# Four modulation rows: summed on the tensor engine in 32-column tiles and spread by DMA, and one operand difference moved from VectorE to GpSimd

## The chip, the core and the metric

The kernel runs on one core of a Trainium2 chip. The metric is the device time of one execution in microseconds (us). The core has five engines that each run their own instruction stream in order and meet through semaphores: TensorE (PE in the profile, with its weight loads as PEld), VectorE (DVE), ScalarE (ACT), GpSimd (POOL) and SyncE (SP), which here only issues DMAs. All matrix products write to PSUM; VectorE and ScalarE read PSUM, GpSimd does not in this kernel.

## What is computed

One transformer block for 2048 tokens of width 576, conditioned on a vector `c`. Everything is float32.

```python
mod = (silu(c) @ w_mod).reshape(1, 6, 1, 576)
sa, ca, ga, sb, cb, gb = (mod[:, i] for i in range(6))
h = layernorm(x) * (1 + ca) + sa
x = x + ga * attention(h)          # 32 query heads of width 18, one shared key/value head, then @ wo
h = layernorm(x) * (1 + cb) + sb
y = layernorm(h)
x = x + gb * (gelu(y @ w1 + b1) @ w2 + b2)   # hidden width 4608
```

The six vectors `sa ... gb` are rows of 576 numbers: one product of `silu(c)` with a slice `w_mod[:, 576 j : 576 (j + 1)]` each. The change concerns four of them: `ga` (j = 2), `sb` (3), `cb` (4) and `gb` (5). The other two are made in the first 20 us in another way and are not touched.

## The kernel before

**Stages.** From 0 to about 125 us: layernorm, queries, keys, values and the first score maxima. From about 125 to 1390 us: attention in 32 "quads" of four heads times 512 tokens (8 quads for each block of 512 tokens, `NQT` = 32). From 1390 to 2241 us: the MLP in 36 steps `v` (18 groups of 256 hidden units, first for one pair of token blocks, `v` = 0 to 17, then for the other pair, `v` = 18 to 35). Each step makes the two products of a 2 x 2 block matrix scheme with seven block products (`A11 S2 S3 A12 S1 A22 S4`), and their operands are sums and differences of blocks of the normalized activations.

**The order in a quad** is written by hand: the strings `QUAD` and `QUADW` list S (score products, line 901, exponentials on ScalarE, line 903), M (score maxima for the next quad, line 319, reduced on VectorE, line 923), X and R (another piece of the maxima), V (the product of probabilities with the values, line 891: four matmuls with 32 output columns each, one for each head of the quad, which write four 32-partition strips of one PSUM bank). PSUM tiles rotate: four named `psB`, three `psM`, one `psC`. After every second key block (every second `kc`, eight times in a quad) `between` takes one step of a generator from the queue `fill`. The first generator in that queue is `late_weights` (from line 493).

**`late_weights`** makes the four rows. For each row, `wmod[j]` is loaded as five blocks of 128 x 576 (line 527 for j = 5, 2, 3; line 92, `load_mod`, for j = 4). GpSimd multiplies each by its column of `silu(c)` (`scaled`, line 498) and adds the five blocks up (`added`, line 501), so that one 128 x 576 tile remains whose sum over the 128 partitions is the row. `bcast` (line 516) makes that sum and copies it to all partitions at once: a matmul with a 128 x 128 matrix of ones (`unity`), in two halves of 288 columns (line 521), each into a `psB` tile of its own, and VectorE scales, adds a constant and writes the result (line 522), to `gab` (`ga`) or to a row of `BC` (0: `sb`, 1: `1 + cb`, 2: `gb / 2`). The loop from line 532 runs 12 steps of `late_weights`: two steps of the sums each, and from the seventh on, in each second one, one `bcast`. Then `wmod[4]` and `wo` are loaded, the sum and the `bcast` for j = 4 follow, and GpSimd multiplies `wo` by `gab` and splits it in two parts (lines 550 to 552), one of five blocks a step.

**Who uses the rows.** `gab`: line 550 at once. `BC[:, 2]`: the preparation of the MLP's weights (line 799), which starts in the fifth quad. `BC[:, :2]`: the second layernorm, from the second token block on.

**The change of pairs.** In the step `v` = 17 the operands of the other pair are formed by `form` (line 1010), a few at a time between the block products. `+X` copies an operand to its rounded form (ScalarE, line 1023), `-X` makes the rest that rounding left out (VectorE or GpSimd, line 1025), and `=X` makes an operand as a difference of two blocks of `yr` (line 1016): `=T3`, `=T4` and `=T1`. `=T4` overwrites the block that `-B21` reads, so it comes after it. Here `e2` is GpSimd; at the first pair (`v` = 0) `e2` is VectorE. While this goes on, TensorE finishes the output products of step 16 (`fc2`, line 1248), whose `psA` tiles (two in rotation) are added to the residual by VectorE at line 1285; the gelu of each block runs over lines 1120, 1121 (ScalarE), 1123 (VectorE), 1124 (ScalarE), 1126 (VectorE), 1129 (ScalarE) and 1132 (GpSimd); lines 1380, 1389 and 1402 add block products on VectorE.

Of the kernel before, what the change touches and what calls it, by code (L numbers as in the profile page):

```python
# [8 lines left out]
F32 = mybir.dt.float32  # L9
F32R = mybir.dt.float32r  # L10
AF = mybir.ActivationFunctionType
ALU = mybir.AluOpType
AX = mybir.AxisListType

S, D, H, DH, F = 2048, 576, 32, 18, 4608
# [17 lines left out]
def block_kernel(ctx: ExitStack, tc, x, wqkv, wo, w1, b1, w2, b2, c, wmod, ident_in, out):  # L33
    nc = tc.nc
    ve, ac, po, pe, sy = nc.vector, nc.scalar, nc.gpsimd, nc.tensor, nc.sync

    per = ctx.enter_context(tc.tile_pool(name="per", bufs=1))
    dr = ctx.enter_context(tc.tile_pool(name="dr", bufs=1, space=bass.MemoryType.DRAM))
# [14 lines left out]
    def psB(): return PS["t"].tile([128, 512], F32, name="psB", bufs=PS["b"])  # L53
# [3 lines left out]
    def big(): return per.tile([128, 10, 512], F32R, name="big", bufs=3)  # L57

    def bigw(n):
        return per.tile([128, KD, n], F32, name="bigw", tag="big", bufs=3, padded_shape=[128, KD, 1024])  # L60
# [14 lines left out]
    BC = per.tile([128, 3, D], F32, name="BC")  # L75
# [14 lines left out]
    def load_mod(j):  # L90
        t = bigw(D)
        sy.dma_start(t, wmod[j])
        return t
# [18 lines left out]
    unity = pa.tile([128, 128], F32, name="unity")  # L112
# [373 lines left out]
    px = pxp.__enter__()  # L486
# [3 lines left out]

    WO, YR, ATT, B2 = {}, {}, {}, {}

    def late_weights():

        gab = pb.tile([128, D], F32, name="gab", tag="r2", bufs=3)

        def scaled(w, k0, k1):
            po.tensor_tensor(w[:, k0:k1], w[:, k0:k1], st[:, k0:k1, None].to_broadcast([128, k1 - k0, D]), op=ALU.mult)

        def added(w, k0, k1, n=1):  # L500
            po.tensor_tensor(w[:, k0:k0 + n], w[:, k0:k0 + n], w[:, k1:k1 + n], op=ALU.add)

        def total(w):

            scaled(w, 0, 2)
            yield
            scaled(w, 2, 4)
            yield
            scaled(w, 4, 5)
            added(w, 0, 2, 2)  # L510
            yield
            added(w, 0, 1)
            added(w, 0, 4)
            yield

        def bcast(w, dst, add, scl):

            for h2 in range(2):
                cs = slice(288 * h2, 288 * (h2 + 1))
                p = psB()  # L520
                pe.matmul(p[:, :288], unity, w[:, 0, cs], start=True, stop=True)
                ve.tensor_scalar(dst[:, cs], p[:, :288], scl, add, op0=ALU.mult, op1=ALU.add)
            yield

        m3, m2, m5 = (bigw(D) for _ in range(3))
        for j, t in ((5, m5), (2, m2), (3, m3)):
            sy.dma_start(t, wmod[j])
        yield
        sums = (x for t in (m5, m2, m3) for x in total(t))
        rows = (x for a in ((m5, BC[:, 2, :], 0.0, 0.5), (m2, gab, 0.0, 1.0), (m3, BC[:, 0, :], 0.0, 1.0))  # L530
                for x in bcast(*a))
        for i in range(12):
            for _ in range(2):
                next(sums, None)
            if i > 5 and i % 2:
                next(rows)
            yield
        m4 = load_mod(4)
        wor = bigw(D)
        sy.dma_start(wor, wo)  # L540
        ATT[0] = big()
        yield
        yield from total(m4)
        yield
        yield
        yield from bcast(m4, BC[:, 1, :], 1.0, 1.0)
        wos = pw.tile([128, 2, KD, D], F32R, name="wos", tag="wA", padded_shape=[128, 2, KD, WQC])
        WOH, WOL = WO["h"], WO["l"] = wos[:, 0], wos[:, 1]
        for k in range(KD):
            po.tensor_mul(wor[:, k, :], wor[:, k, :], gab)  # L550
            po.tensor_copy(WOH[:, k, :], wor[:, k, :])
            po.tensor_tensor(WOL[:, k, :], wor[:, k, :], WOH[:, k, :].bitcast(F32), op=ALU.subtract)
            yield
# [312 lines left out]
    P, PVt = {}, {}  # L866
    posts = []
    fill = deque([late_weights()])

    def step(q):  # L870
# [79 lines left out]
    for n in range(NQT):  # L950
# [13 lines left out]
        for tok in order:  # L964
            if tok[0] == "V":
                g = int(tok[1])
                while g:
                    i = min(g, 4 - pq % 4)
# [36 lines left out]
    def op_pieces(R, e2):  # L1005


        at = {"B11": (0, 0, ve), "B21": (2, 2, e2), "B22": (4, 7, e2), "T2": (6, 5, ve), "T1": (8, 5, ve),
              "T3": (10, 0, ve), "T4": (12, 2, e2), "t0": (0, 4, ve), "t1": (1, 9, ve)}
        less = {"T3": (5, 0, 0), "T4": (2, 5, 2), "T1": (7, 5, 5)}  # L1010

        def form(what):
            for w in what.split():
                if w[0] == "=":
                    x, y, o = (R[:, i:i + 2] for i in less[w[1:]])
                    (e2 if w == "=T1" else ve).tensor_tensor(o, x, y, op=ALU.subtract)
                    continue
                a, r, e = at[w[1:]]
                n = 2 if w[1] in "BT" else 1
                o, lo = (OP, 14) if n == 2 else (TL[0], 2)  # L1020
                hi, src = o[:, a:a + n], R[:, r:r + n]
                if w[0] == "+":
                    ac.activation(hi, src, AF.Copy)
                else:
                    e.tensor_tensor(o[:, lo + a:lo + a + n], src, hi.bitcast(F32), op=ALU.subtract)
        return form
# [31 lines left out]
    px = ctx.enter_context(tc.tile_pool(name="mx", bufs=1, side="right", reuse_waits="tile"))  # L1058
# [256 lines left out]
    for v in range(NV):  # L1315
# [44 lines left out]
        bc = psB()  # L1360
# [111 lines left out]
```

## Time and profile before

| | us |
|---|---|
| median of 3 runs (2241.82 to 2245.19) | 2242.26 |
| the profiled execution's own time | 2243.08 |
| its span, which the profile divides up | 2241.3 |

The profile is of one execution; its times count from the start of the span, so the execution's own time is 1.8 us more than its span. The granted clock of TensorE was 0.998 over the span.

| engine | busy, us | share of the span |
|---|---|---|
| PE | 2212.7 | 99% |
| PEld | 1442.2 | 64% |
| DVE | 1940.8 | 87% |
| ACT | 1645.1 | 73% |
| POOL | 1524.7 | 68% |

Matmuls are pipelined and their ends are modelled, so that PE counts as busy nearly always; where it loses time is read from the starts of its rows. In a row of the timeline stand the start in us, the time from the first start to the last end in us, the engine, the line, the operation, the tile written and the tiles read, for matmuls the rows and columns of the weights, the shape and the count; in brackets the engine's idle time before the row and what ended it. In a row of the table of windows stand the window, its length, and for each engine the busy time and the number of instructions.

### The profile page before, as it was taken

The numbers are of one execution on the slowest core, as the hardware profiler recorded it, in microseconds if no ns is written. First come the engines' busy times: TensorE is split into PE (matmuls) and PEld (weight loads), VectorE is DVE, ScalarE is ACT, GpSimd is POOL, SyncE is SP. The second block draws the span as 40 slices with busy tenths as digits, with TensorE's granted clock in tenths as the row PEclk, the third lists the DMA queues.
The fourth block names the chain that finished last, engine by engine and source line by source line (L and its number), as shares of the span: only waits on it lengthen the run. The fifth ranks groups of instructions, "written<-read, shape, count | busy, mean of one in ns | idle before, by whom it ended". The sixth has DMA issues, their size and how long they took to land.

```text
span 2241.3 us, 45781 instructions
## 1 busy us (share of the span) xinstructions
PE 2212.7 (99%) x16458; PEld 1442.2 (64%) x16458; DVE 1940.8 (87%) x3420; ACT 1645.1 (73%) x3145; POOL 1524.7 (68%) x1760
## 2 busy tenths in 40 slices
PE   7999999999999999999999999999999999999999
PEld 5644544444444544444444445888888888989898
DVE  7589999999999999999999982887888878888787
ACT  5569999999999999999999997444545544344443
POOL 6654356776877787777776300888888857877776
PEclk9999999999999999999999999999999999999999
DMA  6232034443433333343333101666666646676664
GB/s 229 85 129 75 15 114 138 133 142 110 138 121 126 121 122 115 124 139 115 117 127 127 49 13 48 194 177 179 180 178 176 190 122 181 182 213 191 177 183 125
DMA packets 182404, 303.79 MB, mean 136 GB/s; under 512 B 19243, under 2 KB 74923, under 8 KB 182177
## 3 DMA queue, kind: packets, MB, share of 16 engines
q1 hardware_dynamic: 182033, 300.72, 42.9%
q8 instruction: 130, 2.13, 0.4%
q14 instruction: 97, 0.79, 0.1%
q10 hardware_dynamic: 144, 0.15, 0.0%
HBM read 198.71 MB, written 93.19 MB: 130 GB/s over the span
## 4 chain that ended last, share of the span: by engine, by line
PE 86%; DVE 3%; ACT 3%; POOL 2%; issue 1%; DMA 0%; SPq 0%; POOLq 0%; ACTq 0%
PE psC L891 21%; PE psB L1111 18%; PE psA L1214 16%; PE psB L901 13%; PE psM L319 10%; PE psB L700 2%; ACT P L903 2%; PE psB L911 2%; DVE mx L923 1%; PE psA L1248 1%; PE psA L700 1%; DVE xc L921 0%; PE psB L155 0%; PE psB L357 0%; PE psB L248 0%
## 5 line engine op out<-in xcount | busy, mean ns | idle before, releaser
L903 ACT ACTIVATE P<-psB 128x512 f32<-128x512 f32 x2008 | 1043.8, 619 | 35.0 <-PE psM L319 12.3
L923 DVE TENSOR_REDUCE mx<-psM 128x1 f32<-128x512 f32 x1476 | 938.1, 683 | 37.5 <-PE psM L319 14.9
L319 PE MATMUL psM<-KS,qst 64*128 64x512 f32 x1722 | 601.2, 442 | 0.4 <-DVE mx L923 0.4
L901 PE MATMUL psB<-qst,KS 64*128 64x512 f32 x2008 | 585.1, 429 | 1.7 <-DVE mx L337 1.5
L891 PE MATMUL psC<-P,V 128*32 128x256 f32 (+3 forms) x6424 | 576.3, 448 | 0.5 <-ACT O L715 0.5
L901 PEld LDWEIGHTS psB<-qst,KS 64*128 64x128 f32 x2008 | 303.4, 185 | 218.2 <-ACT P L903 141.3
L1111 PE MATMUL psB<-ops,w1a 128*128 128x512 f32 x1512 | 393.8, 396 | 0.2 <-DVE h L1126 0.2
L319 PEld LDWEIGHTS psM<-KS,qst 64*128 64x128 f32 x1722 | 275.6, 184 | 161.9 <-DVE mx L923 120.4
L1111 PEld LDWEIGHTS psB<-ops,w1a 128*128 128x128 f32 x1512 | 270.1, 188 | 46.6 <-DVE h L1126 0.6
L891 PEld LDWEIGHTS psC<-P,V 128*32 128x32 f32 x6424 | 140.0, 108 | 200.1 <-issue 173.4
L1220 DVE TENSOR_TENSOR XT<-psA,XT 128x576 f32<-128x576 f32 x330 | 241.7, 753 | 19.0 <-PE psA L1214 13.6
L1214 PEld LDWEIGHTS psA<-w2s,big 128*128 128x128 f32 x1584 | 223.0, 188 | 13.9 <-POOL big L1188 2.5
L1214 PE MATMUL psA<-w2s,big 128*128 128x288 f32 x1584 | 230.4, 294 | 0.0
L1124 ACT ACTIVATE psB<-gs 128x512 f32<-128x512 f32 x144 | 86.7, 602 | 130.0 <-DVE gs L1123 130.0
L1188 POOL TENSOR_TENSOR big<-s,big 128x512 fp32r<-128x512 f32 x132 | 170.9, 1295 | 10.6
L1120 ACT ACTIVATE h<-psB,b1t 128x512 f32<-128x512 f32 x144 | 97.9, 680 | 102.5 <-PE psB L1111 81.8
L921 DVE CUSTOM_DVE_ANT_0 xc<-psM,xc 128x512 f32<-128x512 f32 x246 | 165.8, 680 | 3.6 <-PE psB L901 1.5
L914 ACT ACTIVATE xc<-psB 128x512 f32<-128x512 f32 x246 | 152.8, 621 | 8.8 <-PE psM L319 7.4
L735 POOL TENSOR_TENSOR os<-O,os 128x512 fp32r<-128x512 f32 x28 | 36.1, 1289 | 164.8 <-ACT os L734 164.8
L1123 DVE SCALAR_TENSOR_TENSOR gs<-psB,h 128x512 f32<-128x512 f32 x144 | 98.5, 684 | 39.5 <-ACT psB L1121 39.4
L762 POOL TENSOR_TENSOR r<-r,r 128x256 fp32r<-128x256 f32 (+1 forms) x162 | 121.6, 751 | 13.0
L1129 ACT ACTIVATE big<-h 128x512 fp32r<-128x512 f32 x39 | 24.7, 633 | 133.7 <-DVE h L1126 133.7
(214 smaller groups left out, 3341.2 us busy)
## 6 DMA issues: line engine op xcount, KB each, us to landing
w1a<-w1scr SPq DMA_DIRECT2D x252, 256.0 KB
w2s<-w2sum SPq DMA_DIRECT2D x132, 288.0 KB
w1scr<-r SPq DMA_DIRECT2D x126, 256.0 KB
w2s<-w2scr SPq DMA_DIRECT2D x76, 288.0 KB
w2scr<-r SPq DMA_DIRECT2D x72, 288.0 KB
w2sum<-r SPq DMA_DIRECT2D x72, 288.0 KB
qst<-qscr SPq DMA_DIRECT2D x192, 72.0 KB
w1a<-w2scr SPq DMA_DIRECT2D x33, 288.0 KB
```

The lines of the kernel that those rows point to most:

```text
L319: pe.matmul(o, QST[n][64 * g:64 * g + 64, p, 128 * qt:128 * (qt + 1)], KS[64 * g:64 * g + 64, 512 * kb:512 * (kb + 1)], start=True, stop=True)
L762: po.tensor_tensor(o[:, n:2 * n], src, o[:, :n].bitcast(F32), op=ALU.subtract)
L891: pe.matmul(PVt[n][32 * j:32 * (j + 1), cs], V[:, kc, :], t[:, j, cs], start=(kc == 0 and h0 == 0), stop=(kc == 15), skip_group_check=True)
L901: pe.matmul(t, KS[64 * g:64 * g + 64, 128 * kc:128 * (kc + 1)], QST[n][64 * g:64 * g + 64, i, :], start=True, stop=True)
L903: ac.activation(P[n, kc][:, 2 * i + g, :], t, AF.Exp, scale=SCALE)
L914: ac.activation(XC[-1], t, AF.Relu)
L921: ve.tensor_tensor_reduce(c, t, c, 1.0, -3.0e38, ALU.add, ALU.max, o)
L923: ve.tensor_reduce(o, t, axis=AX.X, op=ALU.max)
L1111: pe.matmul(o, x, y, start=(first and i == 0), stop=(i == len(terms) - 1), skip_group_check=True)
L1188: po.tensor_tensor(unit(u, 1), x, unit(u, 0).bitcast(F32), op=ALU.subtract)
L1214: pe.matmul(p[:, i, :288], x[:, ts_], W2S[k][:, y], start=(bool(first) and q == 0), stop=(q == 2), skip_group_check=True)
L1220: ve.tensor_tensor(o, p[:, :, :288], o, op=ALU.add)
```

## The change

Four edits, in the code's order. A row of DRAM is set aside for each of the four vectors. `bcast` is rewritten: in place of two matmuls of 128 output columns by 288 it issues four of 32 output columns by 144, the j-th for the j-th quarter of the row, into the j-th 32-partition strip of one `psB` tile (the form that line 891 has); VectorE evacuates 128 x 144 into a small tile; one DMA writes one partition of each strip, 4 x 144 numbers, to the DRAM row; after a `yield`, another DMA reads that row into all 128 partitions of the target. Since `bcast` now yields twice, the loop steps it in each of its last six rounds instead of in each second one. And in `form`, `=T4` goes to `e2` as `=T1` does, so only `=T3` stays on VectorE.

```diff
+    rowscr = [dr.tile([1, D], F32, name="rowscr%d" % n) for n in range(4)]
...
-        def bcast(w, dst, add, scl):
-
-            for h2 in range(2):
-                cs = slice(288 * h2, 288 * (h2 + 1))
-                p = psB()
-                pe.matmul(p[:, :288], unity, w[:, 0, cs], start=True, stop=True)
-                ve.tensor_scalar(dst[:, cs], p[:, :288], scl, add, op0=ALU.mult, op1=ALU.add)
+        def bcast(n, w, dst, add, scl):
+
+            p = psB()
+            for j in range(4):
+                pe.matmul(p[32 * j:32 * (j + 1), :144], unity[:, :32], w[:, 0, 144 * j:144 * (j + 1)], start=True, stop=True,
+                          skip_group_check=True)
+            r = px.tile([128, 144], F32, name="bc", tag="r" + "3543"[n], padded_shape=[128, (256, 256, D, 256)[n]])
+            ve.tensor_scalar(r, p[:, :144], scl, add, op0=ALU.mult, op1=ALU.add)
+            sy.dma_start(rowscr[n].rearrange("o (j c) -> (o j) c", j=4), r.rearrange("(j p) c -> j p c", p=32)[:, 0, :])
+            yield
+            sy.dma_start(dst, rowscr[n].to_broadcast([128, D]))
             yield
...
-            if i > 5 and i % 2:
+            if i > 5:
                 next(rows)
...
-                    (e2 if w == "=T1" else ve).tensor_tensor(o, x, y, op=ALU.subtract)
+                    (ve if w == "=T3" else e2).tensor_tensor(o, x, y, op=ALU.subtract)
```

In the calls of `bcast` the number n of the row is added as the first argument. The tile `bc` takes the place of a tile of the weight preparation that is not used before the fifth quad.

What this moves shows in the order of the instructions. First TensorE in the first quad, where the row of j = 5 is made. Before (KS and qst are keys and queries, P the probabilities, V the values, bigw the summed tile):

```order
L891 MATMUL psC<-P,V 32x256 x4
L521 MATMUL psB<-bigw,unity 128x288 x2
L319 MATMUL psM<-KS,qst 128x512
L901 MATMUL psB<-qst,KS 128x512 x2
L319 MATMUL psM<-KS,qst 128x512
```

And in the changed kernel, where line numbers are six higher there (897 for 891, 907 for 901):

```order
L907 MATMUL psB<-qst,KS 128x512 x2
L319 MATMUL psM<-KS,qst 128x512 x2
L897 MATMUL psC<-P,V 32x256 x4
L522 MATMUL psB<-bigw,unity 32x144 x4
L907 MATMUL psB<-qst,KS 128x512 x2
L319 MATMUL psM<-KS,qst 128x512
L907 MATMUL psB<-qst,KS 128x512 x2
L319 MATMUL psM<-KS,qst 128x512
L897 MATMUL psC<-P,V 32x384 x4
```

The row's matmuls come one step of `fill` earlier than before, and as before directly behind matmuls of the values; the rows of j = 2 and 3 move likewise, that of j = 4 keeps its place.

Second the DMA queue of SP over the first two quads. Before (qst<-ms and qst<-qscr are query loads, big<-os attention outputs, the line 92 and 540 loads `wmod[4]` and `wo`):

```order
L364 DMA qst<-ms 1x8x128 x4
L315 DMA qst<-qscr 18x2x512 x6
L92 DMA bigw<-in_wmod 128x5x576
L540 DMA bigw<-in_wo 128x5x576
L364 DMA qst<-ms 1x8x128 x4
L739 DMA big<-os 18x2x512 x4
L315 DMA qst<-qscr 18x2x512 x6
L364 DMA qst<-ms 1x8x128 x4
```

In the changed kernel:

```order
L526 DMA rowscr_1275<-bc 4x144
L315 DMA qst<-qscr 18x2x512 x6
L528 DMA BC<-rowscr_1275 128x576
L526 DMA rowscr_1276<-bc 4x144
L528 DMA gab<-rowscr_1276 128x576
L526 DMA rowscr_1277<-bc 4x144
L528 DMA BC<-rowscr_1277 128x576
L92 DMA bigw<-in_wmod 128x5x576
L546 DMA bigw<-in_wo 128x5x576
L364 DMA qst<-ms 1x8x128 x4
```

Six row DMAs now stand in the queue ahead of the load of `wmod[4]`, and one of them ahead of a query load.

Third the change of pairs. VectorE before (line 1016 is `=T4`, XT the residual, opt a tail operand):

```order
L1126 SCALAR_TENSOR_TENSOR h<-psB,h 128x512
L1016 TENSOR_TENSOR yr<-yr 128x1024
L1285 TENSOR_TENSOR XT<-psA,XT 128x576 x2
L1123 SCALAR_TENSOR_TENSOR gs<-psB,h 128x512
L1402 TENSOR_TENSOR psB<-psB,u 128x512
L1126 SCALAR_TENSOR_TENSOR h<-psB,h 128x512
L1285 TENSOR_TENSOR XT<-psA,XT 128x576
L1025 TENSOR_TENSOR opt<-yr,opt 128x512
```

GpSimd there in the changed kernel (line 1031 is line 1025 of before, 1138 is 1132, 1022 is 1016):

```order
L1138 TENSOR_TENSOR w1a<-h,gt_20999 128x512
L1031 TENSOR_TENSOR ops<-yr,ops 128x1024
L1138 TENSOR_TENSOR big<-h,big 128x512
L1022 TENSOR_TENSOR yr<-yr 128x1024
L1138 TENSOR_TENSOR big<-h,big 128x512
L1022 TENSOR_TENSOR yr<-yr 128x1024
L1031 TENSOR_TENSOR ops<-yr,ops 128x1024 x2
```

The first of the two line 1022 rows is `=T4`, new on GpSimd between two gelu pieces; the second, `=T1`, was there before. On VectorE the row of line 1016 is gone and the others stand as they did.

More of the change, by code (lines that the diff above doesn't have):

```diff
@@ L529, in late_weights @@
         sums = (x for t in (m5, m2, m3) for x in total(t))
-        rows = (x for a in ((m5, BC[:, 2, :], 0.0, 0.5), (m2, gab, 0.0, 1.0), (m3, BC[:, 0, :], 0.0, 1.0))
+        rows = (x for a in ((0, m5, BC[:, 2, :], 0.0, 0.5), (1, m2, gab, 0.0, 1.0), (2, m3, BC[:, 0, :], 0.0, 1.0))
                 for x in bcast(*a))
@@ L545, in late_weights @@
         yield
-        yield from bcast(m4, BC[:, 1, :], 1.0, 1.0)
+        yield from bcast(3, m4, BC[:, 1, :], 1.0, 1.0)
         wos = pw.tile([128, 2, KD, D], F32R, name="wos", tag="wA", padded_shape=[128, 2, KD, WQC])
```

## The prediction

> **What bounds the kernel now.** The page first: the chain of work that ended last, by engine.
>
> ```profile
> PE 86%; DVE 3%; ACT 3%; POOL 2%; issue 1%; DMA 0%; SPq 0%; POOLq 0%; ACTq 0%
> ```
>
> TensorE carries it. So I ask of each edit what it takes off TensorE's stream at its own place, and whether TensorE catches on something else behind it. Both places are short; the table of windows and the timeline give them.
>
> The first is the start of the attention. A quad's last value matmul is followed on ScalarE by one row of line 715. Four of these rows, here the first and the last, cut the table of windows into three quads that issue the same score, maximum and value work:
>
> ```profile
> 173.39 0.63 ACT L715 ACTIVATE O<-psC 128x512 f32<-128x512 f32 x1
> 290.70 0.62 ACT L715 ACTIVATE O<-psC 128x512 f32<-128x512 f32 x1
> ```
>
> ```profile
> 173.39:214.60 41.21, 41.21 (x375) 20.26 (x375) 39.55 (x77) 37.32 (x77) 11.06 (x9) 1.00 0.31 100
> 214.60:253.32 38.72, 38.72 (x367) 19.21 (x366) 37.65 (x73) 37.08 (x76) 18.51 (x16) 1.00 0.05 12
> 253.32:290.70 37.38, 37.38 (x363) 18.55 (x362) 36.55 (x71) 36.96 (x76) 11.58 (x11) 1.00 0.16 46
> ```
>
> The third quad holds no `bcast` and takes 37.38 us. The second holds one and takes 1.34 us more; the first holds two and most of a third and takes 3.83 more, 1.28 each. So four rows cost 5.17 us, none of it hidden: 36.55 to 36.96 us of 37.38 are busy on VectorE and ScalarE too, so no engine has room for it. TensorE's timeline says how much of that is the matmuls themselves (the row of j = 2, then other places of the first quad):
>
> ```profile
> 175.30 1.06 PE L891 MATMUL psC<-P,V 128*32 128x512 f32 x8
> 176.30 0.49 PE L911 MATMUL psB<-KD,qst 64*128 64x512 f32 x1
> ...
> 183.24 0.64 PE L891 MATMUL psC<-P,V 128*32 128x256 f32 x8
> 183.81 1.24 PE L521 MATMUL psB<-bigw,unity 128*128 128x288 f32 x4
> 184.97 0.42 PE L891 MATMUL psC<-P,V 128*32 128x128 f32 x8
> ...
> 190.40 0.86 PE L891 MATMUL psC<-P,V 128*32 128x128 f32 x16
> 191.19 0.50 PE L319 MATMUL psM<-KS,qst 64*128 64x512 f32 x1
> ```
>
> From start to start, 183.81 to 184.97, line 521 holds TensorE for 1.16 us. The rest, 1.29 - 1.16 = 0.13 us a row, is what the two `psB` tiles and VectorE's evacuation behind it cost others.
>
> The second place is the change of pairs. From 1808 us to the end the table of waits knows one cause that holds TensorE, and the timelines of TensorE, VectorE and GpSimd show its time and chain:
>
> ```profile
> 1800.76 0.63 PE L1111 MATMUL psB<-opt,w1a 128*128 128x512 f32 x2
> 1801.22 0.56 PE L1248 MATMUL psA<-w2s,gt 128*128 128x288 f32 x3
> ...
> 1805.81 0.62 PE L1111 MATMUL psB<-opt,w1a 128*128 128x512 f32 x2
> 1807.69 0.66 PE L1248 MATMUL psA<-w2s,big 128*128 128x288 f32 x3 [1.26 <-DVE XT L1285]
> ```
>
> ```profile
> 1803.16 0.69 DVE L1126 SCALAR_TENSOR_TENSOR h<-psB,h 128x512 f32<-128x512 f32 x1
> 1804.66 2.31 DVE L1016 TENSOR_TENSOR yr<-yr 128x1024 f32<-128x1024 f32 x1 [0.81 <-POOL ops L1025]
> 1806.89 1.41 DVE L1285 TENSOR_TENSOR XT<-psA,XT 128x576 f32<-128x576 f32 x2
> ```
>
> ```profile
> 1802.21 2.41 POOL L1025 TENSOR_TENSOR ops<-yr,ops 128x1024 fp32r<-128x1024 f32 x1
> 1804.59 1.29 POOL L1132 TENSOR_TENSOR big<-h,big 128x512 fp32r<-128x512 f32 x1
> 1811.00 1.68 POOL L1132 TENSOR_TENSOR big<-h,big 128x512 fp32r<-128x512 f32 x1 [5.12 <-ACT big L1129]
> ```
>
> Read from the right: the output product at 1807.69 waits for a `psA` tile that VectorE frees at line 1285; VectorE stands in `=T4` (line 1016) until then, and had waited 0.81 us before it for GpSimd's `-B21`, which reads what `=T4` overwrites.
>
> **The rows, part by part.** *TensorE.* Line 891 shows how long matmuls of 32 output columns take, a group of eight records (four matmuls, two records each), from start to start: 0.57 us for 256 columns (183.24 to 183.81) and 1.00 for 512 (175.30 to 176.30), that is 1.68 ns a column and 0.14 fixed. The group of 16 at 190.40 is one of 128 and one of 256 columns (each value group of a quad adds up to 512); it takes 0.79, so 128 columns behind another group add 0.22, the 128 x 1.68 ns alone. The four new tiles have this form and stand directly behind a value group in all four places, so I take 144 x 1.68 ns = 0.24 us. Bounds: 0.24 below, as the columns must stream; above, 0.38 if the fixed part comes again. That the tiles do not overlap at all is the first rival.
>
> The Trainium skill has a rule against this: "TensorE: Matmul & The Clock Gate", section "Part 3: Packing small matmuls — row/col tiling", says that weight loads overlap running matmuls only where their row groups differ, and four column tiles share all rows. By that rule the eight loads would stand bare, and what that gives is the first rival's time; the row at 190.40 speaks against it, since its second group with eight loads adds nothing beyond its columns.
>
> *VectorE.* Two evacuations of 288 columns become one of 144:
>
> ```profile
> 184.60 0.94 DVE L522 TENSOR_SCALAR gab<-psB 128x288 f32<-128x288 f32 x2
> ```
>
> By proportion 0.94 x 144 / 576 = 0.24 us, certainly between that and 0.47 (one of today's two). VectorE gets back some 0.6 us a row, and the rotation of `psB` gives up one tile instead of two; still I let the 0.13 us a row stay, with bounds of 0 and twice as much. A row then costs 0.24 + 0.13 = 0.37, and 4 x (1.29 - 0.37) = **3.7 us** go; bounds 4 x (1.29 - 0.38 - 0.26) = 2.6 and 4 x (1.29 - 0.24) = 4.2.
>
> *Order.* Three rows come one step of `fill` earlier, 41.21 / 8 = 5.2 us. TensorE stalls there if GpSimd's sum isn't ready. The first of the three sums ends at 150.1 and the last at 171.8 us:
>
> ```profile
> 144.44 5.68 POOL L501 TENSOR_TENSOR bigw<-bigw 128x1152 f32<-128x1152 f32 x3
> ...
> 166.17 5.67 POOL L501 TENSOR_TENSOR bigw<-bigw 128x1152 f32<-128x1152 f32 x3
> ```
>
> The row at 183.81 goes to about 178.6, its neighbours, two steps before and behind, to 168 and 189: the sums are ready 17 us ahead. GpSimd's `wo` blocks come a step later; GpSimd is busy for 11 to 19 us of these quads, and `wo` is not used before the ninth quad.
>
> *DMA.* SP now waits in turn for VectorE's evacuation and for the row to reach DRAM, and what stands behind it waits too. The query load at 169.00 waits at most for an evacuation near 169, which costs it next to nothing. The load of `wmod[4]` is the one that moves:
>
> ```profile
> 131.74 2.00 SPq L527 DMA_DIRECT2D bigw<-in_wmod  x3
> ...
> 169.00 5.58 SPq L315 DMA_DIRECT2D qst<-qscr  x6
> 174.69 0.60 SPq L92 DMA_DIRECT2D bigw<-in_wmod  x1
> ...
> 139.21 5.28 POOL L498 TENSOR_TENSOR bigw<-bigw,st 128x1152 f32<-128x1152 f32 x3 [10.59 <-DMA bigw<-in_wmod]
> 205.74 4.17 POOL L498 TENSOR_TENSOR bigw<-bigw,st 128x1152 f32<-128x1152 f32 x2
> 213.43 5.65 POOL L501 TENSOR_TENSOR bigw<-bigw 128x1152 f32<-128x1152 f32 x3
> ```
>
> It goes from 174.69 to about 194: third evacuation near 191, plus the row's way to DRAM, for which no row stands here and I allow 3 us; the time it may take is bounded in the last rival. Such a load took 7.5 us from issue to use (131.74 to 139.21), so it is there at about 201.5, and GpSimd, which asks at 205.74 less some 3, doesn't wait. The spread rows themselves arrive long before their users. Cost: nothing, covered by GpSimd's idle time.
>
> **The change of pairs.** `=T4` leaves VectorE, and so does its wait: VectorE goes from line 1126 at 1803.16 straight to line 1285 at 1803.85 instead of 1806.89. Without a wait an output product starts 0.46 us after the pair of tail matmuls ahead of it (1800.76 to 1801.22), so the one at 1807.69 would start at 1805.81 + 0.46 = 1806.27: **1.4 us** go. GpSimd does `=T4` from 1805.88 (end of the piece at 1804.59) for 2.4 us, as its row of the same size at 1802.21 takes, to 1808.3; its next piece at 1811.00 then comes some 2 us earlier, for its gelu chain is freed on VectorE, and finds GpSimd idle. What is late next is nothing on TensorE: no other wait follows in that table. Bounds 0 and 1.4.
>
> A rule of the Trainium skill weighs against this move: "SBUF — State Buffer", section "Who interferes with whom", lets an operation of VectorE with two SBUF inputs block while GpSimd reads SBUF. The trace agrees: line 1016 took 2.31 us beside GpSimd. But VectorE's next operations there take one input from PSUM; by the rule only the tail operand behind them could lose about 1 us, and TensorE doesn't wait for it, so the sum stays.
>
> **The sum.** 3.7 + 1.4 = 5.1 us, made against the profiled execution: span 2241.3 to 2236.2, its own time 2243.08 to 2238.0. The median of the runs is 0.8 us below that execution, so I forecast 2242.26 - 5.1 = **2237.2 us**.
>
> **Rivals.** *The tiles don't overlap, their weight loads stand bare*: a weight load of this form takes 108 ns in the row below, eight of them 0.86 us, with 0.24 for the columns 1.10 in place of 1.16. Then 4 x 0.06 + 1.4 = 1.6 us are left: 2240.6. For it: this shape was never run; against it: line 891.
>
> ```profile
> L891 PEld LDWEIGHTS psC<-P,V 128*32 128x32 f32 x6424 | 140.0, 108 | 200.1 <-issue 173.4 <-ACT O L715 10.9 <-ACT P L903 1.1
> ```
>
> Chance 0.1. *`=T4`'s wait only moves*, to GpSimd's pieces or to the operands of step 18: then 3.7 us are left, 2238.6. For it: GpSimd's line 1132 at 1811.00 feeds the output products of step 17, which TensorE now reaches 1.4 us sooner; against it: that piece too comes sooner, by some 2 us. Chance 0.15. *SP holds up `wmod[4]`, and the time ends above before*: GpSimd needs 13.3 us for that sum (205.74 to 219.08) and TensorE asks for the row at 233.59, some 2.8 us earlier then:
>
> ```profile
> 233.59 1.24 PE L521 MATMUL psB<-bigw,unity 128*128 128x288 f32 x4
> ```
>
> From a landing at 217.5 each further us stalls TensorE by one; at 222.6 the gain is eaten, at 227 the time is 2246.7. That takes 33 us from issue to landing in place of 7.5. Chance 0.05, any other loss of this kind with it.
>
> **How the numbers follow.** Forecast 0.7, rivals 0.1, 0.15, 0.05. About 0.2%, 4.5 us, is what a measurement of this kernel can tell from no change; the bound is 2237.8. The forecast's own spread, 2.6 to 4.2 plus 1.4 at most and the runs' scatter of about 1 us, puts four fifths of its 0.7 below it: faster 0.55. The rest and the first two rivals are within: 0.40. Slower 0.05. The range: from 4.2 + 1.4 = 5.6 and 1 us of scatter, 2235.6, to the serial tiles and a little scatter, 2241.0.
>
> **What would show it.** Right: in the windows cut at line 715 the first two quads come near 38.2 and 37.8 us; four groups of eight records of 128*32 by 144, each about 0.24 us from start to start; no idle bracket on line 1248's (then 1254's) product near 1802; GpSimd with two rows of line 1022. Wrong: the groups take about 1 us; TensorE's sequencer waits for GpSimd at the rows, above all at that of j = 4; the bracket comes back with another name. A quad that stays above 39 us with short groups would mean that VectorE, not TensorE, set the 5.17 us.

## The result and the profile after

The changed kernel takes 2237.51 us (median of 12 runs, 2235.57 to 2239.35) beside 2242.09 us for the kernel before (12 runs, 2240.18 to 2245.31): a ratio of 0.9979, 95% interval 0.9971 to 0.9987. The forecast was 2237.2 us, in a range of 2235.6 to 2241.0. The profiled execution took 2238.06 us with a span of 2236.3 us; the forecast span was 2236.2. The line numbers are now six higher, as in the section on the change.

First the chain of work that ended last, by engine. TensorE still carries it, and SP's DMA queue, which got eight more DMAs, has no share that shows:

```profile
PE 87%; DVE 3%; ACT 2%; POOL 2%; issue 1%; DMA 0%; SPq 0%; POOLq 0%; ACTq 0%; DVEq 0%
```

The start of the attention, cut as in the prediction at the ScalarE row that follows a quad's last value matmul, and the table of windows between these rows (window, length, then busy time and instructions of PE, PEld, DVE, ACT and POOL):

```profile
173.40 0.60 ACT L721 ACTIVATE O<-psC 128x512 f32<-128x512 f32 x1
286.46 0.62 ACT L721 ACTIVATE O<-psC 128x512 f32<-128x512 f32 x1
```

```profile
173.40:211.23 37.83, 37.83 (x379) 18.93 (x378) 36.95 (x73) 37.06 (x76) 10.62 (x8) 1.00 0.40 131
211.23:249.08 37.85, 37.85 (x371) 18.80 (x370) 36.85 (x72) 37.09 (x76) 15.03 (x13) 1.00 0.07 20
249.08:286.46 37.38, 37.38 (x363) 18.50 (x362) 36.54 (x71) 36.98 (x77) 15.08 (x14) 1.00 0.15 42
```

The quads of 41.21 and 38.72 us have become 37.83 and 37.85; the third, without a row, has its 37.38 as before. Two rows (j = 2 and 3) fall into the first window and one (j = 4) into the second. So the two cost 0.45 us together, 0.23 each, and the one 0.47, where a row cost 1.29 before. The forecast was 38.2 and 37.8 us for these quads: the first came out 0.4 lower. The first row that is made, that of j = 5, lies ahead of the windows and is priced below.

TensorE's timeline at the first and the third row:

```profile
167.31 0.64 PE L897 MATMUL psC<-P,V 128*32 128x256 f32 x8
167.76 0.43 PE L522 MATMUL psB<-bigw,unity 128*32 128x144 f32 x8
168.12 0.50 PE L907 MATMUL psB<-qst,KS 64*128 64x512 f32 x2
...
188.10 0.43 PE L897 MATMUL psC<-P,V 128*32 128x128 f32 x8
188.34 0.43 PE L522 MATMUL psB<-bigw,unity 128*32 128x144 f32 x8
188.59 0.61 PE L897 MATMUL psC<-P,V 128*32 128x256 f32 x8
```

Between two value groups (188.34 to 188.59) the four tiles hold TensorE for 0.25 us. Ahead of a score product it is 0.36 from start to start (167.76 to 168.12), but there the value group hands over 0.11 early: both together take 0.81 us, 0.57 for the value group alone and 0.24 for the row. VectorE's evacuations (shortest, median and longest, in ns):

```profile
L525 DVE TENSOR_SCALAR bc<-psB x4: 296/297/298, 168.6 to 230.8; 128x144 f32<-128x144 f32 x4
```

0.30 us, between the 0.24 and 0.47 of the prediction. SP's queue:

```profile
177.75 0.52 SPq L526 DMA_DIRECT2D rowscr<-bc  x1
179.34 0.35 SPq L528 DMA_DIRECT2D gab<-rowscr  x1
189.71 0.51 SPq L526 DMA_DIRECT2D rowscr<-bc  x1
191.30 0.31 SPq L528 DMA_DIRECT2D BC<-rowscr  x1
191.66 0.93 SPq L92 DMA_DIRECT2D bigw<-in_wmod  x1
192.69 0.60 SPq L546 DMA_DIRECT2D bigw<-in_wo  x1
200.55 3.38 SPq L364 DMA_DIRECT2D qst<-ms  x4
```

The way of a row to DRAM holds SP for 1.6 us (177.75 to 179.34; I had allowed 3), and `wmod[4]` is issued at 191.66 (forecast: about 194). GpSimd finds it there: its row on it shows no bracket.

```profile
202.36 4.17 POOL L500 TENSOR_TENSOR bigw<-bigw,st 128x1152 f32<-128x1152 f32 x2
```

At the change of pairs, the timelines of TensorE, GpSimd and VectorE:

```profile
1802.21 0.63 PE L1117 MATMUL psB<-opt,w1a 128*128 128x512 f32 x2
1802.68 0.57 PE L1254 MATMUL psA<-w2s,big 128*128 128x288 f32 x3
...
1807.47 1.80 PE L1117 MATMUL psB<-ops,w1a 128*128 128x512 f32 x7
```

```profile
1801.00 1.29 POOL L1138 TENSOR_TENSOR big<-h,big 128x512 fp32r<-128x512 f32 x1
1802.25 2.40 POOL L1022 TENSOR_TENSOR yr<-yr 128x1024 f32<-128x1024 f32 x1
1804.91 1.28 POOL L1138 TENSOR_TENSOR big<-h,big 128x512 fp32r<-128x512 f32 x1 [0.26 <-ACT big L1135]
```

```profile
1799.56 0.69 DVE L1132 SCALAR_TENSOR_TENSOR h<-psB,h 128x512 f32<-128x512 f32 x1
1800.17 1.59 DVE L1291 TENSOR_TENSOR XT<-psA,XT 128x576 f32<-128x576 f32 x2
...
1805.16 1.58 DVE L1031 TENSOR_TENSOR opt<-yr,opt 128x512 fp32r<-128x512 f32 x1
```

The product follows the tail pair after 0.47 us, VectorE goes from line 1132 straight to line 1291, and `=T4` (line 1022) stands on GpSimd. Its next piece waits 0.26 us for ScalarE, not for `=T4`. From the tail pair to the first product of step 18 it now takes 5.26 us (1802.21 to 1807.47); before, with the start at 1805.81, it was 6.86:

```profile
1812.67 0.63 PE L1111 MATMUL psB<-ops,w1a 128*128 128x512 f32 x2
```

That is 1.60 us less. From 1803 us to the end the table of waits of TensorE has one short row left (total, times, longest):

```profile
PE psA L1254 <- DVE XT L1291: 0.2, 1, 0.2
```

### The profile page after: what moved, and what is told of

The parts are those of the page before. It is cut to its first block, busy times and chain, and to the rows that moved or that the text cites. A ratio compares the mean times of both kernels' runs of the same rounds, so it can differ in the third digit from the quotient of the medians.

```text
span 2236.3 us, 45822 instructions
## 1 busy us (share of the span) xinstructions
PE 2210.7 (99%) x16474; PEld 1440.7 (64%) x16474; DVE 1936.0 (87%) x3415; ACT 1645.6 (74%) x3145; POOL 1529.1 (68%) x1761
## 4 chain that ended last, share of the span: by engine, by line
PE 87%; DVE 3%; ACT 2%; POOL 2%; issue 1%; DMA 0%; SPq 0%; POOLq 0%; ACTq 0%; DVEq 0%
PE psC L897 21%; PE psB L1117 18%; PE psA L1220 16%; PE psB L907 13%; PE psM L319 10%; PE psB L706 2%; ACT P L909 2%; PE psB L917 2%; PE psA L1254 1%; DVE mx L929 1%; PE psA L706 1%; DVE xc L927 0%; PE psB L155 0%; PE psB L357 0%; PE psB L248 0%
```

## The experiments

**The measure.** Single executions differ by up to 4 us before the attention begins, in code that all these kernels share: its first exponential on ScalarE starts at 127.90 us in one experiment (both_old) and at 131.88 in another (t4_only).

```profile
127.90 0.60 ACT L909 ACTIVATE P<-psB 128x512 f32<-128x512 f32 x1 [2.55 <-PE psB L907]
```

```profile
131.88 0.60 ACT L903 ACTIVATE P<-psB 128x512 f32<-128x512 f32 x1 [2.85 <-PE psB L901]
```

So the stage of the rows is measured inside the trace, from that first exponential to the first of the fifth quad. The expectations use this; the first 16 exponentials, ahead of any row, still scatter by 0.6 us, so the last column starts at the 17th. There, kernels whose rows are the same agree within 0.08 us. From the 17th to the first ScalarE row of line 721 (715 before) it is 32.43 us in the changed kernel (140.97 to 173.40) and 31.81 in the kernel before (141.58 to 173.39). The row of j = 5 falls into that stretch in the changed kernel only, so it costs 0.62 us there. With the 0.92 of the windows, the four rows now cost 1.54 us, 0.38 each on average.

| kernel | from the 1st, us | from the 17th, us |
|---|---|---|
| before | 157.04 | 145.23 |
| after | 153.48 | 141.59 |
| rows_only (no `=T4` move) | 153.60 | 141.67 |
| t4_only (only the `=T4` move) | 157.42 | 145.25 |
| t4_behind | 153.72 | 141.60 |
| pe_old | 156.63 | 144.95 |
| dve_old | 155.37 | 143.52 |
| both_old | 158.36 | 146.76 |
| serial | 156.15 | 143.95 |
| pe_old_act | 156.50 | 144.89 |
| act_evac, act_evac_5 | 152.61, 152.60 | 141.04, 141.03 |
| old_places | 155.37 | 143.39 |
| old_early | 153.53 | 141.67 |

All edits below are made to the changed kernel, but for t4_only.

**The two parts apart.** rows_only takes the last edit of the change back; t4_only is the kernel before with that edit alone:

```diff
-                    (e2 if w == "=T1" else ve).tensor_tensor(o, x, y, op=ALU.subtract)
+                    (ve if w == "=T3" else e2).tensor_tensor(o, x, y, op=ALU.subtract)
```

> The change with =T4 put back on VectorE, so the new rows alone. Theory (two separate savings that add): the first two quads take 37.8 us each as in the changed kernel, the time is 3.6 us below before (ratio 0.9984), and the stall ahead of the output product at the change of pairs is back with 1.4 us. Rival (the stall at the change of pairs depends on what came earlier): the stall has another size, and the two parts measured apart don't add up to 4.6 to 5.0 us.

> The kernel before with =T4 on GpSimd alone. Theory: the first two quads stay at 41.2 and 38.7 us, the output product at the change of pairs starts 0.47 us after the tail pair ahead of it instead of 1.88, and the time is 1.4 us below before (ratio 0.9994, less than the runs can tell from no change). Rival (the wait goes elsewhere on TensorE): the product starts early, but the gap between the two kernels' TensorE rows 20 us later is below 1 us.

Beside 2242.29 us for the kernel before, rows_only took 2239.52 (ratio 0.9987, 0.9978 to 0.9996) and t4_only 2241.02 (0.9994, 0.9985 to 1.0003). The medians lie 2.77 and 1.27 us below, 4.04 together, which is less than the 4.6 to 5.0 expected; with intervals of about 2 us to either side the times can't say whether the parts add. The trace can. The stage carries the rows' part alone: 145.23 to 141.59, **3.64 us**, and only 0.02 of change with `=T4` alone. And the change of pairs carries the other part alone: from the tail pair to step 18 it takes 6.87 us in rows_only, with the wait back, and 5.26 in t4_only, as in the changed kernel. The interval of t4_only holds 1, so its gain is shown by the trace, not by the times. The wait in rows_only:

```profile
1805.67 0.66 PE L1254 MATMUL psA<-w2s,big 128*128 128x288 f32 x3 [1.26 <-DVE XT L1291]
```

**TensorE's part of a row.** In pe_old two full matmuls of 288 columns write one tile, which VectorE still evacuates with 144 columns; three quarters of each row are left out.

```diff
-            for j in range(4):
-                pe.matmul(p[32 * j:32 * (j + 1), :144], unity[:, :32], w[:, 0, 144 * j:144 * (j + 1)], start=True, stop=True,
+            for h2 in range(2):
+                pe.matmul(p[:, :288], unity, w[:, 0, 288 * h2:288 * (h2 + 1)], start=True, stop=True, skip_group_check=True)
```

> The changed kernel with the two matmuls of 128 output columns by 288 again, both into the same psB tile, of which VectorE still reads 144 columns only: three quarters of each row are left out. TensorE's work is that of before, VectorE's and the psB tiles those of the changed kernel. Theory (TensorE sets the cost): a row costs 1.16 us or a little more again, so the first quad (two rows) takes 39.7 us and the second (one row) 38.6 to 38.7. Rival (VectorE's evacuation and the second psB tile made the cost): they stay within 0.4 us of 37.8.

The quads took 39.83 and 38.55 us, and the stage 3.36 us more than in the changed kernel, 0.84 a row. The matmuls hold TensorE as in the kernel before, 1.17 us from start to start:

```profile
176.50 1.24 PE L522 MATMUL psB<-bigw,unity 128*128 128x288 f32 x4
177.67 0.49 PE L906 MATMUL psB<-qst,KS 64*128 64x512 f32 x1
```

**VectorE's part.** dve_old makes the same evacuation three times, 3 x 0.30 us for the 2 x 0.46 of the kernel before:

```diff
-            ve.tensor_scalar(r, p[:, :144], scl, add, op0=ALU.mult, op1=ALU.add)
+            for _ in range(3):
+                ve.tensor_scalar(r, p[:, :144], scl, add, op0=ALU.mult, op1=ALU.add)
```

> The changed kernel with the evacuation of 128 x 144 done three times, 0.9 us of VectorE a row as before the change; TensorE's work stays new. Theory (TensorE sets the cost, VectorE at most the 0.13 us a row): the first quad takes 37.8 to 38.1 us, the second 37.8 to 38.0. Rival (VectorE sets it): 0.6 us more a row, 39.0 and 38.4 us.

The quads took 38.92 and 38.34 us, the stage 1.93 us more, 0.48 a row. This went to the rival: VectorE's time is worth far more here than the 0.13 us a row that the prediction gave it. With only TensorE's work shortened, a row would have kept that much.

**Do the column tiles overlap?** serial puts the four tiles into one and the same strip, so each must follow the last (again three quarters of a row are left out):

```diff
-                pe.matmul(p[32 * j:32 * (j + 1), :144], unity[:, :32], w[:, 0, 144 * j:144 * (j + 1)], start=True, stop=True,
+                pe.matmul(p[:32, :144], unity[:, :32], w[:, 0, 144 * j:144 * (j + 1)], start=True, stop=True,
```

> The changed kernel with all four matmuls of 32 output columns writing the same 32-partition strip, so that they can't run beside each other; VectorE reads 32 partitions of 144 columns, and three quarters of each row are left out. Theory (the column tiles run beside each other): the group takes about 4 x 0.24 us and the fixed part, 1.0 to 1.2 us from start to start in place of 0.35, and the first two quads come to 39.5 to 39.9 and 38.3 to 38.6 us, as with the old matmuls (39.83 and 38.55). Rival (a group is short because its weights have 32 columns): the group stays near 0.35 us and the quads near 37.8.

```profile
169.28 1.14 PE L522 MATMUL psB<-bigw,unity 128*32 128x144 f32 x8
170.35 0.73 PE L907 MATMUL psB<-qst,KS 64*128 64x512 f32 x3
```

The same eight records take 1.07 us from start to start instead of 0.36. The quads took 39.27 and 38.32 us, the stage 2.36 us more. So this is what tiles that don't overlap would have cost, and those of the change do overlap. That 1.07 is near the 1.10 of the prediction's first rival is chance: the rival counted weight loads that stand bare, but in serial the eight matmuls start 0.12 us apart, and the load for the next starts together with each.

**Two costs, added or not?** Until here TensorE's old work seemed to cost 3.36 us, VectorE's 1.93, and both together, in the kernel before, 3.64, as if the two lay beside each other. both_old tests that at the places of the changed kernel (pe_old with three evacuations), pe_old_act moves pe_old's evacuation to ScalarE.

> The changed kernel, at its own places, with both engines' work at its old size: two full matmuls of 128 by 288 a row and 144 columns evacuated three times (so three quarters of each row are left out). Measure, from here on with the scatter of the first 12 us taken out: from the 17th exponential of the attention, ahead of which no row is made, to the first of the fifth quad; 141.59 us in the changed kernel, 144.95 with TensorE's work alone at its old size (0.84 more a row), 143.52 with VectorE's alone (0.48 more). Theory (the two engines work side by side on a row, and a row costs about the larger of the two times: 0.24 to 0.36 us on TensorE and 0.30 on VectorE in the changed kernel, 1.16 and 0.92 here): 144.8 to 145.5 us, about the case with TensorE's work alone. Rival (the two costs add): 144.95 + 1.93 = 146.9, 146.3 or more.

> Two full matmuls of 128 by 288 a row once more (three quarters of each row are left out), with ScalarE in place of VectorE reading the 144 columns. With the short tiles this move to ScalarE gained 0.55 us over the four rows (141.59 to 141.04 from the 17th exponential of the attention to the first of the fifth quad). Theory (a row costs about the larger of TensorE's and VectorE's time): with 1.16 us on TensorE the VectorE time under it is free, and the move gains nothing: 144.75 to 145.15, beside 144.95 with VectorE. Rival (VectorE's part comes on top of TensorE's): 144.95 - 0.55 = 144.4, 144.6 or less.

both_old took 146.76 us, 5.17 more than the changed kernel; 3.36 + 1.93 = 5.29. **The theory fell:** with one tile the costs nearly add over the four rows. They don't add place by place: both_old's first two quads take 40.29 and 39.29 us, 2.46 and 1.44 more than the changed kernel's, where the single parts (pe_old and dve_old) add up to 2.00 + 1.09 = 3.09 and 0.70 + 0.49 = 1.19. So that the sums agree this well is in part chance. pe_old_act, at 144.89, did what the theory said (144.95 with VectorE), so an evacuation of 0.30 us is free under long matmuls, and one of 0.92 isn't. Why then did the kernel before, with the same work on both engines, need 1.53 us less than both_old? The table of instruction groups of VectorE from 164 to 240 us says it (busy time, mean ns of one, idle time ahead of them), for before, both_old, the changed kernel and pe_old:

```profile
L522 DVE TENSOR_SCALAR BC<-psB 128x288 f32<-128x288 f32 x6 | 2.7, 458 | 0.3
L522 DVE TENSOR_SCALAR gab<-psB 128x288 f32<-128x288 f32 x2 | 0.9, 459 | 0.1
```

```profile
L525 DVE TENSOR_SCALAR bc<-psB 128x144 f32<-128x144 f32 x12 | 3.7, 307 | 2.4 <-PE psB L522 1.6 <-issue 0.5
```

```profile
L525 DVE TENSOR_SCALAR bc<-psB 128x144 f32<-128x144 f32 x4 | 1.2, 297 | 0.0
```

```profile
L524 DVE TENSOR_SCALAR bc<-psB 128x144 f32<-128x144 f32 x4 | 1.2, 307 | 2.1 <-PE psB L522 1.6 <-issue 0.5
```

VectorE is busy for 3.6 and 3.7 us on the rows, but stands idle ahead of them for 0.4 us in the kernel before and for 2.4 in both_old. The kernel before had a tile for each half, so VectorE could take the first half while TensorE made the second; in both_old it stands until both are done. The 2.0 us of idle time are enough for the 1.53. But idle time alone isn't the price: pe_old stands idle for 2.1 us too and takes 0.28 us less than the kernel before, so it costs this much only together with the long evacuation. That the second tile is the reason is argued, not shown: no run added it to both_old, and both_old makes its rows at the places of the changed kernel.

**ScalarE in VectorE's place.** act_evac evacuates the changed kernel's tiles on ScalarE; act_evac_5 is the same kernel in eight executions.

```diff
-            ve.tensor_scalar(r, p[:, :144], scl, add, op0=ALU.mult, op1=ALU.add)
+            ac.activation(r, p[:, :144], AF.Identity, scale=scl, bias=float(add))
```

> The changed kernel with ScalarE in place of VectorE reading the four row sums out of PSUM. What is left of a row's cost is about 0.3 us. Theory (TensorE's 0.24 us is nearly all of it, and ScalarE is as full as VectorE): from the first exponential of the attention to the first of the fifth quad 153.5 us, within 0.3. Rival (VectorE still sets a part, 0.5 us for 0.6 of its own as the run with three evacuations says): 152.6 us.

> The changed kernel with ScalarE instead of VectorE reading the four row tiles out of PSUM, timed in rounds. One look gave 152.61 us from the first exponential of the attention to the first of the fifth quad, 0.87 less than the changed kernel. Theory (VectorE sets a part of what is left of a row, 0.2 us each): the measure again within 0.3 of 152.6, and a median 0.04% below that of the changed kernel, so a ratio to the kernel before of about 0.9975, which its interval can't tell from 0.9979. Rival (that look was scatter): the measure at 153.2 us or more.

The stage took 152.61 and 152.60 us, as the second theory had it; 0.3 of that lies in the first 16 exponentials and isn't the rows', and 141.59 - 141.04 = 0.55 us is, 0.14 a row on average. The first two quads take 37.86 and 37.62 us, and from the 17th exponential to the first row of line 721 it is 32.07. So with ScalarE a row costs about the same in every place, 0.26 us for the first, 0.24 each for the next two and 0.24 for the last; with VectorE it was 0.62, twice 0.23 and 0.47. Over the eight executions it took 2236.92 us (2235.2 to 2237.22) beside 2242.46, ratio 0.9972, 0.9962 to 0.9983. The changed kernel's interval overlaps with this, so the times don't tell the two apart; by the trace it is the best version here.

**`=T4` on VectorE, but later.** t4_behind leaves `=T4` on VectorE and puts it behind the next addition in step 17 (line 1022 is as in rows_only):

```diff
+        if v == NG - 1:
+            t_()
+            more("=T4 +t0")
+        else:
+            more("=T4 +t0")
+            t_()
-        more("=T4 +t0")
-        t_()
```

> The changed kernel with =T4 back on VectorE, but behind the first of the two additions that free psA tiles. Theory (VectorE has no room there, so the work must leave it): the output product behind the tail pair starts on time, 0.47 us after it, and TensorE waits instead about 1.4 us for the addition two products on, so that within 10 us nothing is left of the gain. Rival (only the place of =T4 mattered): no wait above 0.3 us on TensorE until the end of the step, the 1.4 us gained.

```profile
1801.85 0.63 PE L1117 MATMUL psB<-opt,w1a 128*128 128x512 f32 x2
1802.32 0.57 PE L1254 MATMUL psA<-w2s,big 128*128 128x288 f32 x3
...
1806.36 0.67 PE L1254 MATMUL psA<-w2s,big 128*128 128x288 f32 x3 [0.67 <-DVE XT L1291]
...
1808.06 2.27 PE L1117 MATMUL psB<-ops,w1a 128*128 128x512 f32 x9
```

The product behind the tail pair is on time, and a later one waits 0.67 us for line 1291 instead. From the tail pair to step 18 it takes 6.21 us, so 0.65 of the 1.60 us is kept. The wait moves when the work stays on VectorE; it goes when the work leaves. The expectation had the whole wait come back, which was too much.

**Places and loads.** old_places makes the first three rows at their old places, with both halves of a row's DMAs in one step:

```diff
-            if i > 5:
+            if i > 5 and i % 2:
                 next(rows)
+                next(rows)
```

> The changed kernel with the first three rows at their old places, both halves of a row in one step, so that SP stands longer in the wait for the row to reach DRAM. Theory (places and SP's waits cost nothing): from the first exponential of the attention to the first of the fifth quad 153.5 us, within 0.4, as in the changed kernel (153.48; before 157.04). Rival (the earlier places were a part of the gain): 154.2 us or more.

143.39 us, 1.80 more than the changed kernel: the rival's size, but by a mechanism that neither named. The first quad takes 40.25 us and the second 37.85, and TensorE catches on a DMA, which it does neither in the kernel before nor in the changed one from 195 to 225 us. TensorE's timeline there, and SP's:

```profile
205.58 0.50 PE L908 MATMUL psB<-qst,KS 64*128 64x512 f32 x1
207.16 0.47 PE L908 MATMUL psB<-qst,KS 64*128 64x512 f32 x1 [1.07 <-DMA qst<-ms]
```

```profile
194.53 0.63 SPq L92 DMA_DIRECT2D bigw<-in_wmod  x1
195.25 0.61 SPq L547 DMA_DIRECT2D bigw<-in_wo  x1
199.82 2.85 SPq L364 DMA_DIRECT2D qst<-ms  x4
```

The small query rows (4 KB) are issued 4.6 us behind `wmod[4]` and `wo` (1440 KB each), and TensorE gets them only when these are through: its two score products stand 1.58 us apart, where such neighbours otherwise follow within 0.35. The second line of the DMA view from 188 to 215 us, GB/s in slices of 0.675 us, shows both loads at about 400 GB/s until some 205 us:

```profile
GB/s 0 0 24 0 0 0 0 0 3 0 102 201 164 263 341 399 396 406 410 410 403 405 379 386 249 112 41 118 21 58 143 152 94 173 146 0 0 0 0 0
```

In the changed kernel the loads are issued at 191.66 and 192.69 and the query rows at 200.55, 8 us later, and nobody waits. The Trainium skill, "DMA: Bandwidth & Descriptors", section "Queues, rings and completion order", has each DMA engine consume the descriptors of an issuing engine's ring in order; the 1.07 us agree with that. Whether the order in the ring or the bandwidth that the loads take holds the query rows up, no run here tells apart.

old_early tests it: the old places, but SP loads `wmod[4]` behind the first row's write and `wo` behind the second's.

```diff
             if i > 5 and i % 2:
                 next(rows)
+                if i == 7:
+                    m4 = load_mod(4)
+                elif i == 9:
+                    wor = bigw(D)
+                    sy.dma_start(wor, wo)
                 next(rows)
...
-        m4 = load_mod(4)
-        wor = bigw(D)
-        sy.dma_start(wor, wo)
```

> The three rows at their old places once more, with both halves of a row in one step, but SP now issues the load of wmod[4] right behind the first row's two DMAs and the load of wo behind the second's, so that these two large loads no longer stand between the third row and the small query rows (qst<-ms) of the third quad. Measure: from the first exponential of the attention to the first of the fifth quad, 153.48 us in the changed kernel, 155.37 with the old places alone. Theory (the old places lose their 1.9 us only because the query rows land behind two late large loads): 153.3 to 153.9 us, and the first query product of the third quad stands without a DMA in its bracket. Rival (the places themselves cost it, for the rows meet fuller engines there): 155.0 us or more, with the bracket gone or not.

```profile
176.79 0.60 SPq L92 DMA_DIRECT2D bigw<-in_wmod  x1
...
186.33 0.60 SPq L547 DMA_DIRECT2D bigw<-in_wo  x1
...
203.00 3.24 SPq L364 DMA_DIRECT2D qst<-ms  x4
```

141.67 us, and no wait for a DMA: the theory held. Of the 1.72 us won back, 1.58 - 0.35 = 1.23 stood in that one gap. The earlier places gain nothing by themselves (141.59); they only pull the two loads out of the way of the query rows.

## Why the prediction was right, step by step

- **TensorE, 1.16 to 0.24 us a row: right.** The four tiles add 0.24 us net. The opposite case is serial, with 1.07 us instead of 0.36. The prediction set a rule of the Trainium skill ("TensorE: Matmul & The Clock Gate", section "Part 3: Packing small matmuls — row/col tiling") against line 891; the runs don't agree with the rule here, by which the loads would have stood bare. pe_old puts the price of the old matmuls at 0.84 us a row, where the difference of the holds is 0.92.
- **The 0.13 us a row that stay: the size was right, its place was not seen.** The whole stage gained 3.64 us, 0.91 a row, for 0.92 forecast, which leaves 0.38. ScalarE in VectorE's place takes 0.14 of that away and leaves 0.24, the columns alone: the rest is VectorE's evacuation. It is an average: the evacuation costs 0.36 us at the first row, nothing at the next two and 0.23 at the last. Why it differs from place to place, no run shows.
- **VectorE gets back 0.6 us a row, worth at most 0.13: mis-sized.** dve_old puts it at 0.48. The prediction let TensorE's matmuls carry the whole gain; with one tile a row and the old evacuation time, about half of it, 1.93 of 3.64 us, would have been lost. The sum came out because the change shortens both, and that it came so near, 0.91 for 0.92 a row, is luck: measured apart, the two parts are worth 0.84 + 0.48 = 1.32 us a row. Nor is one `psB` tile in place of two the help that the prediction took it for: with the old work on both engines, one tile needs 1.53 us more (both_old; that the tile is the reason is argued above).
- **Order: right.** No stall at a row, and the places are worth nothing by themselves (old_early).
- **DMA, "cost: nothing": right in the sum, for too short a reason.** I asked when `wmod[4]` is used, found that GpSimd asks late enough, and did not ask which small loads stand behind it in the queue. The query rows do; with 4.6 instead of 7.9 us between the second large load and them (old_places) 1.8 us are lost.
- **`=T4`, 1.4 us: right, a little small.** It gained 1.60 us, and GpSimd made it when forecast: at 1802.25 here, 0.04 us behind the tail pair's start, where 0.07 was forecast (1805.88 beside 1805.81). Its wait did not move, the second rival. The tail operand of line 1031, beside GpSimd's lines 1138 and 1022, took 1.58 us where the row of before has 0.68 (below), and TensorE did not wait for it; with that the trace agrees with the Trainium skill, "SBUF — State Buffer", section "Who interferes with whom", as the prediction weighed it.

```profile
1810.84 0.68 DVE L1025 TENSOR_TENSOR opt<-yr,opt 128x512 fp32r<-128x512 f32 x1
```

- **The sum.** Inside the trace 3.64 + 1.60 = 5.24 us for 5.1 forecast. The spans differ by 2241.3 - 2236.3 = 5.0 and the medians by 4.58 (interval 2.9 to 6.5 by the ratio's). The two profiled executions differ in stretches that the change doesn't touch, too: the changed kernel's first exponential comes 0.67 us earlier, but from the fifth quad to the tail pair it takes 1519.64 us where before took 1519.00, and this stretch scatters by 1.6 us among the profiled kernels. So that the forecast span came out within 0.1 us (2236.2 for 2236.3) is luck.

## What to carry to other kernels

Where two engines are both full, ask for each what its shorter work is worth alone, by an experiment that restores only that part: a forecast can come out right, by luck, because the change happens to shorten both. When a transfer is moved in a queue, look beyond its own user for the small transfers behind it, since these meet their deadlines only by the margin that the big ones leave. And a wait on a shared engine is not removed by reordering its work if that engine is full for the next microseconds; it went here only when the work moved to an engine that was idle.

## What the runs showed of the hardware

Four tiles of 128 x 32 weights that share all rows overlap as well as the value matmuls do: 1.07 us in one strip, 0.36 from start to start in four. A row's way through DRAM, from the issue of its write to the issue of the read that waits for it, takes 1.6 us. Two 1440 KB loads at about 400 GB/s hold up 4 KB loads issued 4.6 us behind them. And an evacuation of 128 x 144 takes 0.30 us on VectorE and 0.29 on ScalarE:

```profile
176.61 0.29 ACT L525 ACTIVATE bc<-psB 128x144 f32<-128x144 f32 x1
```

It cost 0.14 us a row on the one, on average over four places, and nothing that shows on the other, though both are busy for about 37 of a quad's 37.4 us.
